# Cosine-weighted linear attention followed by a multiplicative FFN on one core: hand-written instruction order, 1 KB load runs and casting weight loads in place of a scheduled program

## Chip, cores, metric

The kernel runs on one core of one Trainium2 chip. The metric is the device time of one execution in microseconds (us); a run of the kernel before is given as the median of three executions. The page of the profile shows one profiled execution, whose times count from its first instruction.

## What is computed

q, k and v have 8 batches, 8 heads, 576 rows of 64. phi(x) is max(x,0) times a cosine weight, and the same times a sine weight, side by side (128 features); the weights depend on the row.

```python
kv  = einsum('bhsf,bhsd->bhfd', phi(k), v);  z = sum(phi(k), axis=2)
x   = (phi(q) @ kv) / (phi(q) @ z + 1e-6)          # -> 4608 tokens x 512
out = ((x @ w1) * (x @ w2)) @ w3 @ w_out           # 512 -> 1024 -> 1024 -> 512, fp32
```

## The kernel before

Matmuls run in bf16. First the weights are prepared: w1, w2, w_out and w3 are loaded in fp32 by SP's queue (L82 to L96) into the pool `wstage`, cast to bf16 by DVE and ACT, w3 is transposed by PE block by block (L101), and w34b = w3 @ w_out is multiplied out (L106) and evicted by ACT (L108). Then the pool `wstage` is closed, and the pools of the attention (`ld`, `phi` and so on) are opened in its place.

`attention(b)` works in five chunks of rows (128, 128, 128, 128, 64). Per chunk, q is loaded by SP's queue (L131) and k and v by POOL's (L132, L133), in runs of 256 bytes (one row of one head). DVE makes the cosine halves (L137, L141), ACT the sine halves (L139, L143), and v is cast into `va` beside a column of ones (L145, L146). PE transposes the eight heads of phi(q) (L151), and DVE copies them to `qpT` (L152). Then PE sums kv over the chunks (L160), ACT and DVE evict it, and per chunk PE multiplies phi(q) by it (L173), DVE divides (L176 to L183), PE transposes the result (L188), and it is copied into `xT4`, all tokens' transposed x (L190).

`ffn(t)` takes 512 tokens: for each of eight column blocks four matmuls with w1 (L199), four with w2 (L202), an ACT copy of the first (L205) and a DVE product (L206); then four output blocks of eight matmuls each (L210), an ACT copy (L213) and a store from ACT's queue. The tiles `ffnps` have two buffers, which the two groups of a block take in turn:

```python
ps_ffn = ctx.enter_context(tc.tile_pool(name="ps_ffn", bufs=2, space=bass.MemoryType.PSUM))
...
            aT = ps_ffn.tile([P, 512], FP32, name="ffnps")
            bT = ps_ffn.tile([P, 512], FP32, name="ffnps")
```

The program is attention(0), ffn(0), attention(1), ffn(1), ..., attention(7), ffn(7), ffn(8), but the order on each engine is set by the scheduler of the language, which may draw instructions forward; engines then run their queues in order.

Of the kernel before, what the change touches and what calls it, by code (L numbers as in the profile page):

```python
# [42 lines left out]
def kernel(  # L43
# [34 lines left out]
    w34b = wpool.tile([P, 8, DM], BF16, name="w34b")

    with tc.tile_pool(name="wstage", bufs=1) as wst:  # L80
        wf1 = wst.tile([P, 4, DFF], FP32, name="wf1")
        nc.sync.dma_start(out=wf1[:], in_=moe_w1.rearrange("(c p) j -> p c j", p=P))  # L82
        nc.vector.tensor_copy(out=w1b[:, 0:2, :], in_=wf1[:, 0:2, :])
        nc.scalar.copy(out=w1b[:, 2:4, :], in_=wf1[:, 2:4, :])
        wf2 = wst.tile([P, 4, DFF], FP32, name="wf2")
        nc.sync.dma_start(out=wf2[:], in_=moe_w2.rearrange("(c p) j -> p c j", p=P))
        nc.vector.tensor_copy(out=w2b[:, 0:2, :], in_=wf2[:, 0:2, :])
        nc.scalar.copy(out=w2b[:, 2:4, :], in_=wf2[:, 2:4, :])
        wouts = wst.tile([P, 8, DM], FP32, name="wouts")
        nc.sync.dma_start(out=wouts[:], in_=moe_w_out.rearrange("(c p) m -> p c m", p=P))  # L90
        woutb = wst.tile([P, 8, DM], BF16, name="woutb")
        nc.any.tensor_copy(out=woutb[:], in_=wouts[:])
        w3T = wst.tile([P, 8, DFF], BF16, name="w3T")
        for jc in range(8):
            w3f = wst.tile([P, DFF], FP32, name="w3f", bufs=2)
            nc.sync.dma_start(out=w3f[:], in_=moe_w3[ts(jc, P), :])  # L96
            w3c = wst.tile([P, DFF], BF16, name="w3c", bufs=2)
            nc.any.tensor_copy(out=w3c[:], in_=w3f[:])  # L98
            pstage = ps_qt.tile([P, 8, 128], BF16, name="pst")
            for lc in range(8):  # L100
                nc.tensor.transpose(pstage[:, lc, :], w3c[:, ts(lc, 128)], identb[:])  # L101
            nc.any.tensor_copy(out=w3T[:, :, ts(jc, 128)], in_=pstage[:])
        for jp in range(8):
            ps34 = ps_ffn.tile([P, 512], FP32, name="ffnps")
            for lc in range(8):
                nc.tensor.matmul(ps34[:, :], lhsT=w3T[:, lc, ts(jp, 128)],  # L106
                                 rhs=woutb[:, lc, :], start=(lc == 0), stop=(lc == 7))
            nc.scalar.copy(out=w34b[:, jp, :], in_=ps34[:, :])  # L108

    xtpool = ctx.enter_context(tc.tile_pool(name="xt", bufs=1))  # L110
    xT4 = xtpool.tile([P, 4, T], BF16, name="xT4")

    ld = ctx.enter_context(tc.tile_pool(name="ld", bufs=3))
    phi = ctx.enter_context(tc.tile_pool(name="phi", bufs=6))
    qtp = ctx.enter_context(tc.tile_pool(name="qtp", bufs=2))
    xb = ctx.enter_context(tc.tile_pool(name="xb", bufs=8))
    sm = ctx.enter_context(tc.tile_pool(name="sm", bufs=4))
    ffnsb = ctx.enter_context(tc.tile_pool(name="ffn", bufs=2))

    def attention(b):  # L120
# [134 lines left out]
```

## Time and profile before

| | us |
|---|---|
| runs (three) | 365.64, 366.74, 370.58; median 366.74 |
| span of the profiled execution | 364.5 |
| PE busy | 295.6 (81%) |
| DVE, ACT, POOL busy | 171.1, 169.8, 72.6 |

No separate time is given for the profiled execution; its span is 2.2 us below the median of the runs. [...] An interval of a few microseconds may show more than one engine busy with the same work, since matmuls are pipelined.

### The profile page before, as it was taken

What the parts mean: (1) busy time and instruction counts of PE and PEld (TensorE: products, weight loads), DVE (VectorE), ACT (ScalarE), POOL (GpSimd) and SP (SyncE); (2) the same over time, 40 slices, a digit from 0 to 9 for tenths busy, and PEclk for the clock granted to TensorE, in tenths of its full rate; (3) what the DMA queues carried; (4) which work ended last, traced back from release to release, by engine and by line L of the source; (5) the groups of instructions that cost most, each with busy time, mean ns of one, the idle gap of its engine ahead of it and who ended that gap; (6) DMA issues with size and microseconds to landing.
All of it is one profiled execution on the core that took longest, in us unless ns stands there. A gap on an engine that the chain in (4) does not pass through costs nothing.

```text
span 364.5 us, 5583 instructions
## 1 busy us (share of the span) xinstructions
PE 295.6 (81%) x2085; PEld 157.5 (43%) x2112; DVE 171.1 (47%) x476; ACT 169.8 (47%) x276; POOL 72.6 (20%) x107
## 2 busy tenths in 40 slices
PE   0059722572999779999999999999899999899996
PEld 0034322462345544474455446446445544544442
DVE  2322043765530867269429617826742732742230
ACT  2376342545533756368339437736542332332322
POOL 0000161433310735216206402801000000000000
PEclk9999955555899859999999999999999999899999
DMA  8975099999923699537934933882102002001103
GB/s 300 397 270 185 22 227 197 201 219 170 177 61 115 151 218 167 150 112 186 178 116 124 227 99 103 187 175 101 32 0 97 22 0 108 9 0 48 69 0 115
DMA packets 51851, 48.60 MB, mean 133 GB/s; under 512 B 39536, under 2 KB 39536, under 8 KB 51824
## 3 DMA queue, kind: packets, MB, share of 16 engines
q1 hardware_dynamic: 40752, 19.93, 24.3%
q0 software_dynamic: 5888, 18.88, 23.3%
q10 hardware_dynamic: 5184, 9.44, 6.9%
q8 instruction: 16, 0.26, 0.4%
q14 instruction: 11, 0.09, 0.1%
HBM read 38.80 MB, written 9.44 MB: 132 GB/s over the span
## 4 chain that ended last, share of the span: by engine, by line
PE 62%; DMA 22%; DVE 6%; ACT 4%; SPq 2%; issue 2%; ACTq 0%; DVEq 0%; POOL 0%; POOLq 0%
PE ffnps L202 17%; PE ffnps L210 16%; PE ffnps L199 16%; DMA qs<-in_q_dram 12%; DMA w3f<-in_moe_w_dram 6%; PE kvA L160 3%; PE xst L188 2%; PE pst L151 2%; PE kvB L160 2%; SPq L96 2%; PE ffnps L106 2%; DVE qpT L152 1%; DMA ks<-in_k_dram 1%; ACT qp L143 1%; DMA vs<-in_v_dram 1%
## 5 line engine op out<-in xcount | busy, mean ns | idle before, releaser
L199 PE MATMUL ffnps<-xT,w1b 128*128 128x512 bf16 x275 | 76.1, 387 | 6.3 <-ACT asb L205 1.8
L206 DVE TENSOR_TENSOR abT<-asb,ffnps 128x512 bf16<-128x512 bf16 x72 | 49.3, 685 | 65.9 <-PE ffnps L202 60.2
L202 PE MATMUL ffnps<-xT,w2b 128*128 128x512 bf16 x280 | 76.9, 384 | 0.4 <-DVE abT L206 0.2
L205 ACT CAST asb<-ffnps 128x512 bf16<-128x512 f32 x72 | 42.1, 584 | 60.6 <-PE ffnps L199 59.0
L210 PE MATMUL ffnps<-w34b,abT 128*128 128x512 bf16 x284 | 63.4, 379 | 0.3
L132 POOL DMA_DIRECT2D ks<-in_k_dram x40 | 35.3, 884 | 84.3 <-ACT w34b L108 42.5
L151 PE MATMUL pst<-identb,qp 128*128 128x128 bf16 (+1 forms) x320 | 29.9, 237 | 19.0 <-DVE qpT L152 9.6
L213 ACT COPY osb<-ffnps 128x512 f32<-128x512 f32 x36 | 21.1, 587 | 51.3 <-PE ffnps L210 45.5
L210 PEld LDWEIGHTS <-abT 128*128 128x128 bf16 x288 | 28.2, 98 | 34.0
L202 PEld LDWEIGHTS <-w2b 128*128 128x128 bf16 x288 | 26.8, 98 | 35.6 <-issue 12.9
L199 PEld LDWEIGHTS <-w1b 128*128 128x128 bf16 x288 | 27.4, 99 | 33.7 <-issue 6.0
L143 ACT ACTIVATE qp<-qs,sinv 128x512 bf16<-128x512 f32 (+1 forms) x40 | 28.9, 721 | 24.4 <-DMA qs<-in_q_dram 20.8
L133 POOL DMA_DIRECT2D vs<-in_v_dram x40 | 34.9, 874 | 21.2 <-ACT va L145 10.3
L152 DVE COPY qpT<-pst 128x1024 bf16<-128x1024 bf16 (+1 forms) x40 | 25.1, 627 | 17.7 <-PE pst L151 17.5
L151 PEld LDWEIGHTS <-qp 128*128 128x128 bf16 (+1 forms) x320 | 22.6, 108 | 24.8 <-issue 10.3
L139 ACT ACTIVATE kp<-ks,sinv 128x512 bf16<-128x512 f32 (+1 forms) x40 | 28.3, 718 | 3.7 <-DMA ks<-in_k_dram 2.7
L188 PE MATMUL xst<-identb,xblk 128*128 128x128 bf16 (+1 forms) x160 | 22.7, 230 | 8.0 <-DVE xblk L180 7.7
L141 DVE TENSOR_SCALAR qp<-qs,cosv 128x512 bf16<-128x512 f32 (+1 forms) x40 | 19.9, 500 | 16.0 <-DMA qs<-in_q_dram 15.8
L160 PEld LDWEIGHTS <-kp 128*128 128x128 bf16 (+1 forms) x320 | 20.4, 102 | 15.4 <-issue 7.5
L137 DVE TENSOR_SCALAR kp<-ks,cosv 128x512 bf16<-128x512 f32 (+1 forms) x40 | 20.8, 519 | 11.5 <-PE kvB L160 8.5
L101 PE MATMUL pst<-identb,w3c 128*128 128x128 bf16 x64 | 5.7, 242 | 23.4 <-DVE w3c L98 21.9
L190 ACT COPY xT<-xst 128x512 bf16<-128x512 bf16 (+1 forms) x26 | 13.8, 532 | 17.9 <-PE xst L188 17.9
(49 smaller groups left out, 243.2 us busy)
## 6 DMA issues: line engine op xcount, KB each, us to landing
out_dram<-osb ACTq DMA_DIRECT2D x36, 256.0 KB, 2.0
qs<-in_q_dram SPq DMA_DIRECT2D x32, 256.0 KB, 5.7
ks<-in_k_dram POOLq DMA_DIRECT2D x32, 256.0 KB, 5.9
vs<-in_v_dram POOLq DMA_DIRECT2D x32, 256.0 KB, 6.5
wf<-in_moe_w_dram SPq DMA_DIRECT2D x2, 2048.0 KB, 9.8
w3f<-in_moe_w_dram SPq DMA_DIRECT2D x8, 512.0 KB, 4.1
wouts<-in_moe_w_out_dram SPq DMA_DIRECT2D x1, 2048.0 KB, 17.0
qs<-in_q_dram SPq DMA_DIRECT2D x8, 128.0 KB, 7.0
```

The costliest lines, as they stand in the source:

```text
L132: nc.gpsimd.dma_start(out=ks[:Rc], in_=k[b, :, s0:s0 + Rc, :].rearrange("h s d -> s h d"))
L133: nc.gpsimd.dma_start(out=vs[:Rc], in_=v[b, :, s0:s0 + Rc, :].rearrange("h s d -> s h d"))
L143: nc.scalar.activation(out=qp[:Rc, :, D:F], in_=qs[:Rc], func=ACTF.Relu, scale=sinv[:Rc, c:c + 1], bias=0.0)
L151: nc.tensor.transpose(pst[:, h, 0:Rc], qp[:Rc, h, :], identb[:Rc, :Rc])
L152: nc.vector.tensor_copy(out=qpT[:, :, s0:s0 + Rc], in_=pst[:, :, 0:Rc])
L160: nc.tensor.matmul(slot, lhsT=kps[c][:Rc, h, :], rhs=vas[c][:Rc, h, :], start=first, stop=last)
L188: nc.tensor.transpose(xst[:, kc, 0:Rc], xblk[:Rc, 2 * kc:2 * kc + 2, :], identb[:Rc, :Rc])
L199: nc.tensor.matmul(aT[:, :], lhsT=w1b[:, kc, ts(jc, 128)], rhs=xT4[:, kc, cols], start=(kc == 0), stop=(kc == 3))
L202: nc.tensor.matmul(bT[:, :], lhsT=w2b[:, kc, ts(jc, 128)], rhs=xT4[:, kc, cols], start=(kc == 0), stop=(kc == 3))
L205: nc.scalar.copy(out=asb[:], in_=aT[:, :])
L206: nc.vector.tensor_mul(out=abT[:, jc, :], in0=asb[:], in1=bT[:, :])
L210: nc.tensor.matmul(ops[:, :], lhsT=abT[:, jc, ts(ms, 128)], rhs=w34b[:, jc, :], start=(jc == 0), stop=(jc == 7))
```

## The change

The order of every engine's instructions is now as the code is written (`tc.manual_schedule()`), and the code is written so that pieces of attention(t+1) stand between the 24 groups of four matmuls of ffn(t). A batch has 25 pieces: five `prep` (no PE work), five kv chunks, five transposes of phi(q), five `num`, five `x_tr`. In tile 0 they begin with the ninth group. attention(0) stands alone ahead of ffn(0). The first 512 rows of a batch are dealt to chunks as rows 4p+j, so that a load run is 1 KB; k, v and q are loaded per batch by SP's queue, one batch ahead; stores leave SP's queue too. The weights come by POOL's queue and are cast by the transfer; w3 @ w_out is made in two halves with `prep(0)` between. `ffnps` has four buffers; the attention's PSUM tile `pnum` has one. v is cast by POOL. The load pool no longer lies where the weights are staged.

```diff
-    ps_ffn = ctx.enter_context(tc.tile_pool(name="ps_ffn", bufs=2, space=bass.MemoryType.PSUM))
+    ld = ctx.enter_context(tc.tile_pool(name="ld", bufs=2))
...
+    ps_ffn = ctx.enter_context(tc.tile_pool(name="ps_ffn", bufs=4, space=bass.MemoryType.PSUM))
+    ps_att = ctx.enter_context(tc.tile_pool(name="ps_att", bufs=1, space=bass.MemoryType.PSUM))
+    ps_tr = ctx.enter_context(tc.tile_pool(name="ps_tr", bufs=2, space=bass.MemoryType.PSUM))
+    ctx.enter_context(tc.manual_schedule())
...
+    for i in range(4):
+        nc.gpsimd.dma_start(out=w3b[:, 0:4, ts(i, 256)], in_=w3v[:, 0:4, ts(i, 256)])
+        nc.gpsimd.dma_start(out=woutb[:, ts(i, 2), :], in_=wov[:, ts(i, 2), :])
...
+    for i in range(2):
+        nc.gpsimd.dma_start(out=w3b[:, 4:8, ts(i, 512)], in_=w3v[:, 4:8, ts(i, 512)])
+    cosv, sinv = _trig_tables(nc, const)
...
+    def load(b):
+        for name, src in (("k", k), ("v", v), ("q", q)):
+            t = ld.tile([P, H, 4, D], FP32, name=name + "s")
+            nc.sync.dma_start(out=t[:], in_=src[b, :, 0:512, :].rearrange("h (p j) d -> p h j d", j=4))
+            t4 = ld.tile([64, H, D], FP32, name=name + "s4")
+            nc.sync.dma_start(out=t4[:], in_=src[b, :, 512:S, :].rearrange("h p d -> p h d"))
...
+    load(0)
+    for i in range(4):
+        nc.gpsimd.dma_start(out=w1b[:, :, cs], in_=w1v[:, :, cs])
+        nc.gpsimd.dma_start(out=w2b[:, :, cs], in_=w2v[:, :, cs])
+    load(1)
...
+    def w34_half(half):
+        for lc in range(8):
+            for jp in range(4):
+                nc.tensor.transpose(pst[:, jp, :], w3b[:, 4 * half + jp, ts(lc, 128)], identb[:])
+            if lc % 2:
+                nc.scalar.copy(out=w3T[:], in_=pst[:, 0:4, :])
+            else:
+                nc.vector.tensor_copy(out=w3T[:], in_=pst[:, 0:4, :])
+            if prev is not None:
+                mms(*prev)
...
+        nc.gpsimd.tensor_copy(out=va[:R, c, :, 0:D], in_=vs)
...
+    def attention_units(b):
+        order = [0, 1, 2, 3, 4] if b % 2 == 0 else [4, 0, 1, 2, 3]
+        u = [(lambda c=c: kv_chunk(b, c)) for c in range(NCH)]
+        u.insert(2, lambda: q_tr(b, order[0]))
+        u.insert(5, lambda: q_tr(b, order[1]))
+        for i in range(NCH + 1):
+            if i < NCH:
+                u.append(lambda c=order[i]: num(b, c))
+            if i + 2 < NCH:
+                u.append(lambda c=order[i + 2]: q_tr(b, c))
+            if i >= 1:
+                u.append(lambda c=order[i - 1]: x_tr(b, c))
...
+    w34_half(0)
+    for c in range(NCH):
+        prep(0, c)
+    w34_half(1)
...
+    for u in attention_units(0):
+        u()
+    for t in range(NT):
+            if b + 1 < B:
+                load(b + 1)
+            first = 8 if t == 0 else 0
+            pr = [(lambda c=c: prep(b, c)) for c in range(NCH)]
+            at = attention_units(b)
+            todo = pr[0:2] + [f for p in zip(pr[2:], at[0:3]) for f in p] + at[3:]
+            per = len(todo) / (n - first)
```

`num` is the product with kv and the division (now three DVE instructions of 128x8, 128x8 and 128x512), `x_tr` the transposes of its result with an ACT copy. A matmul or an eviction of the FFN has the same form as before.

Three places show how the instructions moved. At the start of POOL's queue (w3b, woutb, w1b, w2b are the bf16 weights, s_i the row numbers for the weights of phi) there stood before, from the identity matrix on:

```order
L21 IOTA s_i 128x5
masks.py:197 MEMSET identb 128x128
masks.py:199 AFFINE_SELECT identb<-identb 128x128
L132 DMA ks<-in_k_dram 128x8x64
L133 DMA vs<-in_v_dram 128x8x64
```

and now, behind seven weight transfers and the identity matrix:

```order
L95 DMA woutb<-in_moe_w_out_dram 128x2x512
L99 DMA w3b<-in_moe_w_dram 128x4x512 x2
L26 IOTA s_i 128x4
L27 IOTA s_i 128x1
L106 MEMSET va_137 128x40
L106 MEMSET va_139 128x40
L123 DMA w1b<-in_moe_w_dram 128x4x256
L124 DMA w2b<-in_moe_w_dram 128x4x256
```

The row numbers are now made behind ten transfers, and k and v have left this queue. On DVE, at the end of the tables of cosines and sines, there stood before

```order
L38 TENSOR_TENSOR sinv<-sinv,th 128x5
L87 CAST w2b<-wf_120 128x2048
L98 CAST w3c<-w3f 128x1024 x3
L102 COPY w3T<-pst 128x8x128
L98 CAST w3c<-w3f 128x1024 x4
L146 MEMSET va 128x8
L141 TENSOR_SCALAR qp<-qs,cosv 128x8x64
```

and now

```order
L44 TENSOR_TENSOR sinv<-sinv,th 128x5
L145 COPY w3T<-pst 128x512 x4
L155 CAST w34b<-ffnps 128x512 x2
L175 TENSOR_SCALAR kp<-ks,cosv 128x8x64
L179 TENSOR_SCALAR qp<-qs,cosv 128x8x64
```

The casts of weights are gone, and the first copy of transposed w3 stands behind the tables. On ACT, between two tiles of the FFN (asb and osb are the FFN's evictions, kp and qp the sine halves of phi), there stood before

```order
L163 CAST kvs<-kvA 128x260
L143 ACTIVATE qp<-qs,sinv 128x8x64 x2
L139 ACTIVATE kp<-ks,sinv 128x8x64
L190 COPY xT_325<-xst 128x4x128
L145 CAST va<-vs 128x8x64 x3
L190 COPY xT_325<-xst 128x4x128
L139 ACTIVATE kp<-ks,sinv 128x8x64 x2
L205 CAST asb<-ffnps 128x512
```

and now, within a tile,

```order
L281 CAST asb<-ffnps 128x512
L177 ACTIVATE kp<-ks,sinv 128x8x64
L181 ACTIVATE qp<-qs,sinv 128x8x64
L281 CAST asb<-ffnps 128x512
L177 ACTIVATE kp<-ks_595,sinv 64x8x64
L181 ACTIVATE qp<-qs_603,sinv 64x8x64
L281 CAST asb<-ffnps 128x512 x2
L201 CAST kvs<-pnum 128x260
L281 CAST asb<-ffnps 128x512 x2
```

An eviction of the FFN now stands behind two or four activations of the next batch, and the casts of v are gone.

## Rows read from the trace of the kernel before

**Rows 1.** The page's 40 slices: PE's busy tenths; GB/s moved.

```profile
PE   0059722572999779999999999999899999899996
...
GB/s 300 397 270 185 22 227 197 201 219 170 177 61 115 151 218 167 150 112 186 178 116 124 227 99 103 187 175 101 32 0 97 22 0 108 9 0 48 69 0 115
```

**Rows 2.** Windows: us, busy (count) of PE, PEld, DVE, ACT, POOL; clock; DMA; GB/s.

```profile
20.00:43.40 23.40, 19.77 (x126) 10.60 (x128) 5.55 (x8) 14.31 (x17) 0.00 (x0) 1.00 0.44 146
43.40:92.00 48.60, 19.84 (x190) 15.82 (x191) 25.49 (x76) 21.71 (x34) 20.13 (x23) 0.53 1.13 198
92.00:361.00 269.00, 255.96 (x1769) 131.06 (x1793) 134.69 (x366) 127.02 (x223) 51.68 (x77) 0.97 0.43 104
188.30:198.00 9.70, 8.88 (x122) 6.35 (x121) 8.49 (x29) 8.38 (x15) 3.93 (x9) 1.00 0.43 125
```

**Rows 3.** Timeline of POOL at its first load: start, us, what, [idle <-releaser].

```profile
43.96 1.02 POOL L132 DMA_DIRECT2D ks<-in_k_dram  x1 [42.49 <-ACT w34b L108]
```

**Rows 4.** DMA queues, first 0 to 43.4 us, then 43.4 to 92 us.

```profile
q1 hardware_dynamic: 3248, 10.49, 66.5%
...
q1 hardware_dynamic: 17320, 4.36, 60.6%
q0 software_dynamic: 1616, 5.21, 52.0%
```

**Rows 5.** Timeline of PE within ffn(0).

```profile
97.24 1.03 PE L199 MATMUL ffnps<-xT,w1b 128*128 128x512 bf16 x4
98.25 1.02 PE L202 MATMUL ffnps<-xT,w2b 128*128 128x512 bf16 x4
99.11 1.03 PE L199 MATMUL ffnps<-xT,w1b 128*128 128x512 bf16 x4
```

**Rows 6.** Chain that ended last, output matmuls of one tile.

```profile
273.13 6.91 PE ffnps L210 x32
```

**Rows 7.** Groups by form: names, count | busy, mean ns | idle before, releasers.

```profile
L206 DVE TENSOR_TENSOR abT<-asb,ffnps 128x512 bf16<-128x512 bf16 x72 | 49.3, 685 | 65.9 <-PE ffnps L202 60.2 <-PE ffnps L199 3.6 <-ACT asb L205 1.1
L205 ACT CAST asb<-ffnps 128x512 bf16<-128x512 f32 x72 | 42.1, 584 | 60.6 <-PE ffnps L199 59.0 <-DVE den L178 0.8 <-PE ffnps L202 0.5
L132 POOL DMA_DIRECT2D ks<-in_k_dram x40 | 35.3, 884 | 84.3 <-ACT w34b L108 42.5 <-ACT kp L139 14.6 <-ACT asb L205 6.7
...
L139 ACT ACTIVATE kp<-ks,sinv 128x512 bf16<-128x512 f32 x32 | 22.5, 717 | 3.2 <-DMA ks<-in_k_dram 2.2 <-PE kvB L160 1.0
L152 DVE COPY qpT<-pst 128x1024 bf16<-128x1024 bf16 x32 | 21.7, 679 | 10.9 <-PE pst L151 10.8
...
L180 DVE TENSOR_TENSOR xblk<-numA,den 128x256 bf16<-128x256 f32 x32 | 13.4, 418 | 0.3
...
L178 DVE RECIPROCAL den<-den 128x8 f32<-128x8 f32 x32 | 6.2, 195 | 0.3
...
L32 DVE TENSOR_SCALAR cosv<-cosv 128x5 f32<-128x5 f32 x5 | 0.9, 170 | 0.0
...
masks.py:199 POOL TENSOR_SCALAR_AFFINE_SELECT identb<-identb 128x128 bf16<-128x128 bf16 x1 | 0.3, 295 | 0.1
...
masks.py:197 POOL MEMSET identb<- 128x128 bf16 x1 | 0.2, 200 | 0.0
```

**Rows 8.** Timeline of PE: one chunk's transposes, half of one chunk's products.

```profile
118.07 0.62 PE L151 MATMUL pst<-identb,qp 128*128 128x128 bf16 x8
...
118.52 0.29 PE L173 MATMUL numA<-kvs,qpT 128*128 128x65 bf16 x4
```

**Rows 9.** DVE's cosine half of q: durations, min, median, max.

```profile
L141 DVE TENSOR_SCALAR qp<-qs,cosv x40: 426/478/896, 46.8 to 265.1; 128x512 bf16<-128x512 f32 x32, 64x512 bf16<-64x512 f32 x8
```

**Rows 10.** Timeline of PE: eight transposes of w3, early and later.

```profile
20.86 1.03 PE L101 MATMUL pst<-identb,w3c 128*128 128x128 bf16 x8 [20.86 <-DVE w3c L98]
...
26.31 0.61 PE L101 MATMUL pst<-identb,w3c 128*128 128x128 bf16 x8
```

More of the change, by code (lines that the diff above doesn't have):

```diff
@@ L78 @@
[L78 to L108, printed above, removed]
@@ new lines, with x_tr @@
+    xT = {}
+    def x_tr(b, c):
+        R = ROWS[c]
+        xblk = att[b]["x"].pop(c)
+        xf = xblk[:R].rearrange("p g h d -> p (g h d)")
+        if b % 2 == 0:
+            slot = S * b + 128 * c
+        else:
+            slot = S * b + (0 if c == 4 else 64 + 128 * c)
+        t, o = divmod(slot, 512)
+        if t not in xT:
+            xT[t] = xtp.tile([P, 4, 512], BF16, name="xT")
+        pst = ps_tr.tile([P, 8, 128], BF16, name="pst")
+        for kc in range(4):
+            nc.tensor.transpose(pst[:, kc, 0:R], xf[:, ts(kc, 128)], identb[:R, :R])
+        nc.scalar.copy(out=xT[t][:, :, ds(o, R)], in_=pst[:, 0:4, 0:R])
@@ L195, in ffn, with out_rows, ffn_groups @@
+    def out_rows(g):
+        pair, r = divmod(g, 9)
+        b0 = 2 * pair
+        if r == 4:
+            return [(64 * i, 64, out[ds((b0 + i) * S + 512, 64), :]) for i in range(2)]
+        b, j = (b0, r) if r < 4 else (b0 + 1, r - 5)
+        return [(0, 128, out[ds(b * S, 512), :].rearrange("(p j) m -> p j m", j=4)[:, j, :])]
+    def ffn_groups(t):
+        x = xT[t]
+        abT = fsb.tile([P, 8, 512], BF16, name="abT", bufs=2)
         for jc in range(8):
             aT = ps_ffn.tile([P, 512], FP32, name="ffnps")
+            for kc in range(4):
+                nc.tensor.matmul(aT[:, :], lhsT=w1b[:, kc, ts(jc, 128)], rhs=x[:, kc, :],
+                                 start=(kc == 0), stop=(kc == 3))
+            asb = fsb.tile([P, 512], BF16, name="asb")
+            nc.scalar.copy(out=asb[:], in_=aT[:, :])
+            yield
@@ L197, in ffn @@
             bT = ps_ffn.tile([P, 512], FP32, name="ffnps")
             for kc in range(4):
[L199 removed]
+                nc.tensor.matmul(bT[:, :], lhsT=w2b[:, kc, ts(jc, 128)], rhs=x[:, kc, :],
                                  start=(kc == 0), stop=(kc == 3))
[L201 to L203 removed]
@@ L204, in ffn @@
-            asb = ffnsb.tile([P, 512], BF16, name="asb")
-            nc.scalar.copy(out=asb[:], in_=aT[:, :])
             nc.vector.tensor_mul(out=abT[:, jc, :], in0=asb[:], in1=bT[:, :])
+            yield
         for ms in range(4):
```

269 lines of the change are left out of this document (149 added, 120 removed).

## Prediction

> **What bounds the kernel now.** I read the page's slices first, then busy time by stage, then the timeline where a stage begins and the DMA queues of each stage, and last the groups by form, for prices. In the slices (9.1 us each) the reader sees PE idle in the first two, half busy up to the tenth, and at nine tenths or more in most of the rest [rows 1]. By stage [rows 2]: from 20.0 to 43.4 us the weights are prepared, PE busy 19.8 of 23.4 us. From 43.4 to 92.0 us, where ffn(0) begins, PE is busy 19.8 of 48.6 us at a granted clock of 0.53, nearly always the lower of its levels, while the DMA engines' share is 1.13 (packets overlap, so every engine has work all the time): this stage waits for transfers. From 92.0 to 361.0 us PE is busy 256.0 of 269.0 us at 0.97: PE bounds it. So what can be had lies mostly in the first 92 us; behind them only 13 us are idle.
>
> The second stage starts late because POOL's first load of k waits 42.5 us for the last eviction of w34b [rows 3]: the load tiles lie where the weights were staged. It is slow because of its runs of 256 bytes. While active, SP's queue moved 4.36 MB in 60.6% of 48.6 us, 148 GB/s, and POOL's 5.21 MB in 52.0%, 206 GB/s; the weights before moved 10.49 MB in 66.5% of 43.4 us, 363 GB/s [rows 4].
>
> In the last stage a pair of groups of ffn(0) starts at 97.24 us and the next at 99.11, 1.87 us for eight matmuls [rows 5], where 32 output matmuls take 6.91 us, 0.216 each [rows 6], or 1.73 for eight. The other 0.14 us is the w2 group's wait for a free `ffnps` buffer: with two buffers it needs the product of the pair before, which takes DVE 0.685 us and follows PE [rows 7].
>
> **The change, part by part.** I build the time anew: the start of ffn(0), then PE's work, then the tail.
>
> *Transfers ahead of ffn(0).* Both batches that SP issues at once and POOL's weights share the engines. Ahead of the last piece of w3 stand 4.2 MB of w3, 2.1 MB of w_out and 7.1 MB of q, k, v. A packet of q (252 bytes on average) took 0.606*48.6*16/17320 = 27.2 ns of one engine, one of the weights (3230 bytes) 0.665*43.4*16/3248 = 142 ns [rows 4]. On the line between them 1 KB takes 57 ns (287 GB/s over 16 engines) and 2 KB 97 ns (339 GB/s). So 8.4 MB in 1 KB runs take 29 us, 4.2 MB in 2 KB runs 12, 0.8 MB of 64-row chunks in 256 B runs 5, and the start about 2 (300 against 397 GB/s in the first two slices [rows 1]): w3 is complete at 49 us. That a cast in the transfer costs nothing is not shown by any row. Its ends are 363 and 206 GB/s for POOL's 6.3 MB, the two rates nearest to it; I take the line, since the runs are like those of no row.
>
> *Work under them.* POOL issues ten transfers at 0.88 us [rows 7] ahead of the row numbers, so DVE's tables (27 instructions of 0.17 us or a little over) end at about 15 us, and the first half of w34 starts there, not with its data. ACT's ten activations of `prep(0)`, 7.2 us at 0.717 [rows 7], stand between the halves. Both lie beside the transfers. Behind the last piece of w3 come four rounds of the second half, each of four transposes and four long matmuls: 1.2 us at full clock, nearly twice that at half (eight transposes took 1.03 us early and 0.61 later [rows 10]). At 1.7 us that is 7 us, to 56.
>
> *attention(0)* stands alone. Seven pieces of eight matmuls at 0.6 us [rows 8] and the eviction of kv make 5 us. Then `pnum` has one buffer, so the next `num` waits for the division of the one before: 0.6 us of PE, then add and reciprocal (0.2 each) and a product of 512 elements, for which I take 0.7 (0.418 for 256, nearly all by the element [rows 7]), with handovers 2.0 us. Five of them make 10. ffn(0) starts at 71 us instead of 92. Bounds: were transfers free, DVE's tables, 16 rounds at 1.2, `prep` and attention(0) would still need 15+19+7+15 = 56; with casts at 206 GB/s w3 is complete at 2+25+31 = 58 us, and ffn(0) starts at 80. What was hidden for nothing before, the casts of weights on ACT and DVE, goes, and is worth nothing by itself.
>
> *PE's work from there.* The FFN is 9 tiles of 24 groups at 4*0.216 = 0.864 us, 186.6 us; four buffers remove the 0.14 us per pair, 72 times, 10 us. A batch of attention has 60 transposes at 0.62/8 and 80 products at 0.29/4 us [rows 8], 10.4 us. From below: the last stage has 1769 matmuls [rows 2], 905 of them not of the FFN's 864, of 140 per batch 6.5 batches; 256.0 - 9*(8*1.87+6.91) = 59 us, 9.1 each. I take 9.6, and seven batches are 67 us. For waits at the seams, of which before had 13 us, I take 6.
>
> *The tail* behind PE's last matmul, from 361.0 us to the span's end at 364.5, stays: 3.5 us.
>
> Sum: 71 + 186.6 + 67 + 6 + 3.5 = 334 us of span, against 364.5. The span lies 2.2 us below the median of the runs, so 336 us against 366.74.
>
> *What must stay hidden.* At the head of a tile ACT gets ten activations (7.2 us) and four evictions (2.3 us) in seven groups and their pieces, about 7.2 us of PE: it falls 2.3 us behind. Four buffers let PE run three groups ahead, 2.6 us, so the cover is thin but holds. POOL's cast of v is in no row. Between a memset of 128 elements at 0.20 us (more elements can't take less) and a select of 128 elements at 0.295 [rows 7], 512 elements take 0.2 to 1.2 us; I take 0.8. Five of them end before the chunks' products are due, some 2 us apart. Loads of a batch are issued a tile (30 us) ahead and need 13 us.
>
> **The rivals.** *A: the cast makes the transfer slow.* For it: no row shows one, and q, k, v now take bandwidth from the weights. Against it: POOL's queue held 206 GB/s beside SP's. At half of that, 103, w3 is complete at 2+25+61 = 88, ffn(0) starts at 110, and waits 9 us more for the last chunk of w1 and w2 (4.2 MB, 41 us, to 129): 336+39+9 = 384, slower. It loses against before once w3 lands later than 49+31 = 80 us, which is a cast stream under 119 GB/s; at 206 it gives 345.
>
> *B: queues in order make PE wait in the mixed tiles.* For it: the thin cover on ACT, one `pnum` buffer, DVE's product of the FFN behind `prep`. DVE's cosine halves took 0.43 to 0.90 us [rows 9], so something can nearly double them. Against it: by the prices of rows 7 and 9, ACT has twelve evictions, ten activations and six copies of about 0.5, some 17 us, and DVE eight products, ten halves, five copies and five divisions, some 20, of 30 us per tile. At 2 us more per tile the time is 350, at 5 us 371; from 3.3 us per tile on no gain beyond 2% is left. [...]
>
> *C: the front part stays at half clock.* [...] The trace doesn't bear it out for this mix: in 188.3 to 198.0 us, 122 matmuls, 8.88 us of PE in all and so nearly all of them small, ran at 1.00 [rows 2]. But the stage at 0.53 was one with PE half idle, and w34 with attention(0) is that too. Four rounds at 2.2 and attention(0)'s PE part doubled add 9 us: 345.
>
> **How the numbers follow.** The forecast has 0.64; its own range, 322 to 350, takes ffn(0)'s start from 61 to 80 us, with 9.1 to 10.4 us per batch. A has 0.12 (a third of it the slower end), B 0.16, C 0.08. The time is the forecast's, 336 us. For 8 in 10 the range reaches to B's middle and A's milder end, 318 to 358. About 2% (359.4 us) is what a measurement can tell from no change. Faster: 0.63 of the forecast, 0.06 of A, 0.09 of B, all of C: 0.86. Within 2%: 0.08, from B and A. Slower: 0.06, from A's end and B's.
>
> **What would show it.** Right: SP's first loads at the start and not at 43 us; the last transfer of w3 landing near 49 us; PE's first FFN matmul at 65 to 77; pairs of groups without pieces 1.73 us apart in the last two tiles; 30 to 31 us from tile to tile in between at clock 1.00. Wrong: PE waiting for POOL's transfers beyond 60 us (A), for ACT's asb or POOL's va in every mixed tile (B), clock 0.5 up to ffn(0) with the transfers done (C). A start of ffn(0) at 71 with a time over 350 would mean that the steady tiles are mispriced, not the front.

## The result, and the profile after

The changed kernel takes 308.24 us (median of four runs, 308.13 to 308.85) against 366.50 of the kernel before on the same chip: 0.839 of its time, 95% interval 0.834 to 0.843. The forecast of faster was right, the 336 us were 28 too many, and the time lies below the range of 318 to 358. One of the four runs of the first woven front (the last experiment), its profiled one, lay 1.6% above the fastest and is left out of its median, and no start of ffn(0) is read from it.

By stage (columns as in [rows 2]; the stage up to 55.2 us answers to the first 92 us of [rows 2], the rest to its long third row; a clock of 1.00 is full speed by the profile):

```profile
0.00:55.20 55.20, 29.90 (x266) 17.44 (x268) 22.73 (x69) 16.83 (x28) 20.39 (x38) 0.93 1.18 234
58.00:88.00 30.00, 25.88 (x199) 13.89 (x201) 16.94 (x33) 12.57 (x23) 3.42 (x5) 0.88 0.35 93
...
118.00:148.00 30.00, 27.95 (x241) 15.22 (x244) 18.80 (x42) 16.20 (x29) 2.84 (x5) 1.00 0.63 161
148.00:178.00 30.00, 29.74 (x248) 16.13 (x252) 18.40 (x41) 18.10 (x33) 2.84 (x5) 1.00 0.63 166
```

ffn(0) begins at 55.25 us (timeline of PE) instead of 92.0. Up to there the clock is 0.93 in the mean, not 0.53 as in the second stage before (0.50 in each of its windows from 50 us on). Then PE is busy nearly all the time: a window in which an even batch is worked in (148 to 178) has 0.26 us idle, one with an odd batch (118 to 148) 2.05. The start of the program, in PE's timeline:

```profile
17.02 1.89 PE L133 MATMUL ffnps<-woutb,w3T 128*128 128x512 bf16 x4 [7.82 <-DVE w3T L145]
...
25.31 1.93 PE L133 MATMUL ffnps<-woutb,w3T 128*128 128x512 bf16 x8
28.41 0.62 PE L140 MATMUL pst<-identb,w3b 128*128 128x128 bf16 x8 [1.18 <-DMA w3b<-in_moe_w_dram]
32.39 1.89 PE L133 MATMUL ffnps<-woutb,w3T 128*128 128x512 bf16 x4 [3.35 <-DVE w3T L145]
...
38.05 0.39 PE L140 MATMUL pst<-identb,w3b 128*128 128x128 bf16 x4
...
41.53 1.93 PE L133 MATMUL ffnps<-woutb,w3T 128*128 128x512 bf16 x8
43.30 0.68 PE L196 MATMUL pnum<-va,kp 128*128 128x65 bf16 x16
...
55.25 0.61 PE L278 MATMUL ffnps<-xT,w1b 128*128 128x512 bf16 x1
```

The reader sees four stages: the first half of w34 (17.0 to 27.2), a gap in which DVE and ACT make the features of batch 0, the second half (32.4 to 43.5) and attention(0) (to 55.2). When their data came is seen in the DMA queues from 2 to 33 us, and in the issues of SP and POOL (for an issuing queue, the second column is how long the issue took):

```profile
q0 software_dynamic: 4420, 3.23, 66.3%
q1 hardware_dynamic: 5396, 4.25, 52.5%
```

```profile
17.53 6.87 SPq L116 DMA_DIRECT2D ks<-in_k_dram  x1
...
25.25 8.65 SPq L116 DMA_DIRECT2D vs<-in_v_dram  x1
...
32.87 0.74 POOL L124 DMA_DIRECT2D w2b<-in_moe_w_dram  x1 [3.46 <-DMA w3b<-in_moe_w_dram]
```

q0 are POOL's casting transfers: their bytes are counted as written (bf16), so 3.23 MB were 6.46 MB read (in the whole span q0 has 5.24 MB for the weights, which came as 10.49 MB before [rows 4]). q1 is SP's. Two of SP's issues took 7 to 9 us each while transfers were under way, so that until 33 us only 4.25 MB of q, k, v were moved, and the last issue in POOL's row that waits for w3 is released at 32.87 us. The second half did not wait for that last piece: PE waited until 32.39 us for DVE, whose order puts the features of batch 0 (27.8 to 31.9) ahead of the first copy of transposed w3, and the rounds that use the last piece began only at 38.05.

### The profile page after: what moved, and what is told of

The parts are those of the page before. It is cut to its first block, busy times and chain, and to the rows that moved or that the text cites. A ratio compares the mean times of both kernels' runs of the same rounds, so it can differ in the third digit from the quotient of the medians.

```text
span 306.4 us, 5315 instructions
## 1 busy us (share of the span) xinstructions
PE 265.0 (86%) x2074; PEld 141.8 (46%) x2112; DVE 160.2 (52%) x358; ACT 141.5 (46%) x249; POOL 38.0 (12%) x68
## 3 DMA queue, kind: packets, MB, share of 16 engines
q0 software_dynamic: 8480, 5.24, 11.5%
## 4 chain that ended last, share of the span: by engine, by line
PE 77%; ACT 9%; DVE 6%; issue 4%; DMA 3%; POOL 0%; ACTq 0%; POOLq 0%
PE ffnps L292 20%; PE ffnps L278 18%; PE ffnps L285 17%; PE ffnps L133 6%; PE pst L210 6%; ACT qp L181 4%; PE pnum L218 4%; PE pnum L196 3%; ACT kp L177 3%; DMA woutb<-in_moe_w_out_dram 3%; PE pst L244 2%; ACT asb L281 2%; DVE xblk L225 1%; PE pst L140 1%; DVE kp L175 1%
## 5 line engine op out<-in xcount | busy, mean ns | idle before, releaser
L292 PE MATMUL ffnps<-w34b,abT 128*128 128x512 bf16 x275 | 69.7, 379 | 0.7
L178 POOL CAST va<-vs 128x512 bf16<-128x512 f32 (+1 forms) x40 | 23.3, 626 | 164.1 <-DMA vs<-in_v_dram 138.4
L245 ACT COPY xT<-pst 128x512 bf16<-128x512 bf16 (+1 forms) x40 | 21.7, 544 | 30.4 <-PE pst L244 30.4
L292 PEld LDWEIGHTS <-abT 128*128 128x128 bf16 x288 | 25.0, 98 | 21.3
L210 PE MATMUL pst<-identb,qp 128*128 128x128 bf16 (+1 forms) x320 | 23.4, 217 | 8.8 <-ACT qp L181 8.8
L133 PE MATMUL ffnps<-woutb,w3T 128*128 128x512 bf16 x62 | 19.8, 451 | 11.2 <-DVE w3T L145 11.2
L225 DVE TENSOR_TENSOR xblk<-pnum,den 128x512 bf16<-128x512 f32 (+1 forms) x40 | 27.6, 689 | 1.4
L210 PEld LDWEIGHTS <-qp 128*128 128x128 bf16 (+1 forms) x320 | 18.8, 99 | 16.6 <-ACT qp L181 10.8
L218 PEld LDWEIGHTS <-qpT 128*128 128x128 bf16 (+1 forms) x320 | 14.4, 100 | 15.5 <-DVE xblk L225 6.5
L222 DVE TENSOR_SCALAR den<-pnum 128x8 f32<-128x8 f32 (+1 forms) x40 | 6.5, 163 | 28.1 <-PE pnum L218 28.1
L218 PE MATMUL pnum<-kvs,qpT 128*128 128x65 bf16 (+1 forms) x320 | 17.0, 194 | 4.0 <-DVE xblk L225 2.9
L196 PEld LDWEIGHTS <-kp 128*128 128x128 bf16 (+1 forms) x320 | 15.1, 99 | 10.5 <-issue 4.1
## 6 DMA issues: line engine op xcount, KB each, us to landing
vs<-in_v_dram SPq DMA_DIRECT2D x8, 1024.0 KB, 11.5
qs<-in_q_dram SPq DMA_DIRECT2D x8, 1024.0 KB, 10.7
vs<-in_v_dram SPq DMA_DIRECT2D x8, 128.0 KB, 11.5
```

Source lines behind the costliest of these rows:

```text
L133: nc.tensor.matmul(acc[jp][:, :], lhsT=w3T[:, ts(jp, 128)], rhs=woutb[:, lc, :], start=(lc == 0), stop=(lc == 7))
L210: nc.tensor.transpose(pst[:, h, 0:R], qp[:R, c, h, :], identb[:R, :R])
L218: nc.tensor.matmul(nt[:R, h // 4, ds((h % 4) * 65, 65)], lhsT=qpT[:, h, ds(128 * c, R)], rhs=kvs[:, h, :], start=True, stop=True)
L225: nc.vector.tensor_tensor(out=xblk[:R], in0=n4[:, :, :, 0:D], in1=den[:R].unsqueeze(3).to_broadcast([R, 2, 4, D]), op=ALU.mult)
L292: nc.tensor.matmul(ops[:, :], lhsT=abT[:, jc, ts(ms, 128)], rhs=w34b[:, jc, :], start=(jc == 0), stop=(jc == 7))
```

## The experiments

All runs with a time stand beside the kernel before; the changed kernel's ratio to it is 0.839. Differences in us are of medians. ffn(0)'s start and the distance of tiles are read from PE's timeline (first matmul with w1 of a tile).

### Odd batches in the order of their rows

An odd batch takes its chunks in the order 4, 0, 1, 2, 3, but its features and kv chunks stand in the order 0 to 4: the last feature is the first that is transposed.

```diff
-            pr = [(lambda c=c: prep(b, c)) for c in range(NCH)]
+            pr = [(lambda c=c: prep(b, c)) for c in ([0, 1, 2, 3, 4] if b % 2 == 0 else [4, 0, 1, 2, 3])]
...
-        u = [(lambda c=c: kv_chunk(b, c)) for c in range(NCH)]
+        u = [(lambda c=c: kv_chunk(b, c)) for c in order]
```

> In batches 1, 3, 5, 7 the first piece that transposes phi(q) is of chunk 4, whose activations ACT does last; the trace of the changed kernel has PE waiting 8.8 us in all there, four times. Here the odd batches prepare and sum chunk 4 first. Theory (these waits are real and nothing stands behind them): 308.2 - 8.8 = about 299.5 us, and the four waits gone. Rival (ACT is simply late at the head of a tile, and PE then waits at the next piece instead): 306 to 308 us.

296.71 us, ratio 0.808 [0.803, 0.813]: 11.5 us less than the changed kernel, more than the waits. Why it is more is seen in the changed kernel's PE timeline and windows behind the first of these waits:

```profile
72.39 0.60 PE L210 MATMUL pst<-identb,qp 64*128 64x64 bf16 x8 [3.80 <-ACT qp L181]
72.92 1.89 PE L285 MATMUL ffnps<-xT,w2b 128*128 128x512 bf16 x4
74.61 0.65 PE L196 MATMUL pnum<-va,kp 128*128 128x65 bf16 x8
...
77.21 1.04 PE L210 MATMUL pst<-identb,qp 128*128 128x128 bf16 x8
```

```profile
68.00:72.40 4.40, 0.60 (x4) 0.11 (x3) 2.90 (x7) 4.33 (x8) 0.00 (x0) 0.94 0.00 0
72.40:76.00 3.60, 3.60 (x23) 1.86 (x24) 1.11 (x2) 0.00 (x0) 0.00 (x0) 0.50 0.02 5
```

After the 3.8 us of idleness four long matmuls take 1.7 us from start to next instead of 0.86: the granted clock is 0.50 in the window's row, and the same work takes some 2 us more up to 77.21. In this run the same window is at 1.00. Tile 0 got 5.7 us shorter (36.64 to 30.95), each of the three later tiles with an odd batch 1.6 (28.94 to 27.30), where the wait was 1.7 and the clock did not fall (1.00 from 126 to 130 us, around the first of them). Another 0.5 us lies ahead of ffn(0).

### Two buffers for the FFN's sums

`ps_ffn` has two buffers again, and for that two of the four sums of w34 lie in the two halves of a `pnum` tile.

```diff
-    ps_ffn = ctx.enter_context(tc.tile_pool(name="ps_ffn", bufs=4, space=bass.MemoryType.PSUM))
+    ps_ffn = ctx.enter_context(tc.tile_pool(name="ps_ffn", bufs=2, space=bass.MemoryType.PSUM))
...
-        acc = [ps_ffn.tile([P, 512], FP32, name="ffnps") for _ in range(4)]
+        two = ps_att.tile([P, 2, 512], FP32, name="pnum")
+        acc = [ps_ffn.tile([P, 512], FP32, name="ffnps") for _ in range(2)] + [two[:, 0, :], two[:, 1, :]]
```

> ffnps has two buffers instead of four (half of the sums for w34 lie in the attention's PSUM tile for that). Theory (the four buffers save what the prediction priced, 0.14 us per pair of groups): 72 pairs, +10 us, 318 us, a little less where a piece covers the wait. Rival (the buffers are also the cover for ACT, which falls behind by 2.3 us and more at the head of a tile): +10 and 3 to 5 us in each of seven tiles, 340 to 355 us. Other rival (pieces between the groups hide the wait everywhere but in the last two tiles): 311 us.

315.81 us, ratio 0.861 [0.854, 0.868]: 7.6 us more than the changed kernel. A pair of groups without pieces, here (tile 7) and in the changed kernel (tile 8):

```profile
271.26 1.03 PE L279 MATMUL ffnps<-xT,w1b 128*128 128x512 bf16 x4
272.27 1.02 PE L286 MATMUL ffnps<-xT,w2b 128*128 128x512 bf16 x4
273.13 1.03 PE L279 MATMUL ffnps<-xT,w1b 128*128 128x512 bf16 x4
```

```profile
285.02 1.03 PE L278 MATMUL ffnps<-xT,w1b 128*128 128x512 bf16 x4
285.88 1.03 PE L285 MATMUL ffnps<-xT,w2b 128*128 128x512 bf16 x4
286.74 1.03 PE L278 MATMUL ffnps<-xT,w1b 128*128 128x512 bf16 x3
```

1.87 us with two buffers, 1.72 with four: the forecast's 0.14 per pair, seen alone. That is 1.0 us in each of the last two tiles. In tiles with a batch it is 0.9 us (even) and 0.3 (odd, where PE waits for ACT anyhow), and tile 0 is 0.6 shorter, so over the program the two buffers cost 5.0 us and not 10. The other 2.0 us lie ahead of ffn(0), where the sums of w34 now share `pnum`: that is a price of the edit's second part and not of the FFN's buffers. The bigger loss, ACT falling behind in each tile, didn't come: PE waited 5.0 us in all for `asb`.

### Attention behind the FFN, not between

No piece is placed between the groups; the loop that the kernel has behind them then places all 25 at the tile's end.

> attention(t+1) stands behind ffn(t) on every engine, not between its groups; nothing else is changed. Theory (the pieces' answers from DVE and ACT are hidden by FFN groups): a batch alone takes 12.4 us as attention(0) does, and 2 to 3 us more for the first chunks of prep, against 8.6 us per tile between groups: +6 to 7 us in each of seven tiles, 350 to 357 us. Rival (placement matters little, the kernel before had only 13 us of idle PE with most of its attention apart from the FFN): at most +13, 321 us.

```diff
-                want = min(len(todo), int(round((g + 1 - first) * per)))
+                want = 0
```

398.36 us, ratio 1.086 [1.078, 1.093]: slower than before, and 90 us slower than the changed kernel, twice what the waits alone let expect. One batch alone, and the ffn behind it:

```profile
122.10:138.50 16.40, 11.40 (x140) 9.10 (x142) 8.62 (x21) 8.51 (x15) 2.10 (x4) 0.62 0.82 215
138.50:141.70 3.20, 3.20 (x8) 1.22 (x8) 0.00 (x0) 0.67 (x2) 0.74 (x2) 0.50 0.42 98
```

From its first matmul a batch takes 16.4 us alone, PE idle 5 of them, at a clock of 0.62, and the FFN's first eight matmuls still run at 0.50. Between FFN groups the same pieces ran at 1.00 (the changed kernel's windows from 118 to 178 us). So laying the pieces between the groups saves their waits and here also kept the clock; how much of the 90 us either makes was not measured apart. Whether the low clock of the batch alone comes from its idle time or from its small matmuls, this run doesn't show.

### Runs of 256 bytes again

Chunks of 128 consecutive rows, in four transfers per load.

```diff
-            nc.sync.dma_start(out=t[:], in_=src[b, :, 0:512, :].rearrange("h (p j) d -> p h j d", j=4))
+            for j in range(4):
+                nc.sync.dma_start(out=t[:, :, j, :], in_=src[b, :, ts(j, 128), :].rearrange("h p d -> p h d"))
...
```

The row numbers of the tables and the rows of the stores follow.

> Chunks are again blocks of 128 rows, so q, k, v are loaded in runs of 256 bytes, by four transfers where there was one. Theory (steady tiles hide 3.5 MB at 148 GB/s, 24 of 30 us; in the front the 4.2 MB that stand beside w3 take 28 instead of 16 us): w3 is complete 8 to 12 us later, and the time is 313 to 320 us. Rival (the front is bound by the engines' order, which has slack against the transfers): under 311 us. Rival on the other side (loads don't keep up with the tiles): over 330 us.

325.59 us, ratio 0.887 [0.881, 0.892]: 17.4 us more, all of it ahead of ffn(0) (72.98 instead of 55.25 us), and none in the tiles, whose distances stay within 0.02 us (27.37, 28.95), but for tile 0, which is 0.24 shorter. DMA queues from 2 to 51 us, and the longest waits of PE and, up to 73 us, of DVE:

```profile
q0 software_dynamic: 8480, 5.24, 72.1%
q1 hardware_dynamic: 16612, 4.18, 56.1%
```

```profile
PE ffnps L134 <- DVE w3T L146: 31.0, 2, 23.0
...
DVE qp L180 <- DMA qs<-in_q_dram: 17.8, 4, 16.3
```

All 5.24 MB of the weights were through by then, but SP had moved only 4.18 MB in 49 us, batch 0's 3.5 and little more. It is now not w3 that is late, as the theory had it, but q: DVE waits 16.3 us for it in one piece, its features of batch 0 stand ahead of the copies of transposed w3 in half 1, and PE waits 23.0 us behind them.

### Tables first; batch 1's loads later; batch 1's loads at once

Three runs on the transfers. In the first the tables are made ahead of the weights' issues:

```diff
     identb = const.tile([P, P], BF16, name="identb")
+    cosv, sinv = _trig_tables(nc, const)
     for i in range(4):
...
-    cosv, sinv = _trig_tables(nc, const)
```

> The cosine and sine tables are made ahead of the weight transfers in POOL's and VectorE's order; nothing else moves. In the changed kernel VectorE makes the tables from 11.5 to 16.6 us, behind POOL's ten transfer issues, and TensorE waits 7.8 us for the first evicted w3 tile. Order theory: this wait is what holds half 0 back, so half 0 starts near 11 us instead of 17, ffn(0) at 49 instead of 55.3, and the kernel takes about 302 us. Rival, transfers: half 0 ends with the last w_out piece (landed at 25.25, its matmuls at 25.31), half 1 with the last w3 piece (32.8); these do not move, so ffn(0) stays within 1 us of 55.3 and the time at 307 to 308 us. The POOL issues come some 1 to 2 us later than now, so the transfers may even land later: up to 310.

308.76 us, ratio 0.839 [0.832, 0.845]: nothing. The wait only changes its name. PE's waits up to 60 us, here and in the changed kernel:

```profile
PE pst L140 <- DMA w3b<-in_moe_w_dram: 13.9, 5, 9.5
PE ffnps L133 <- DVE w3T L145: 3.7, 1, 3.7
```

```profile
PE ffnps L133 <- DVE w3T L145: 11.2, 2, 7.8
PE pst L140 <- DMA w3b<-in_moe_w_dram: 9.3, 2, 8.2
```

Half 0 starts earlier, waits for its weights piece by piece, and ends no earlier: its evictions on DVE begin at 28.29 us, in the changed kernel at 26.63.

In the second, batch 1's loads are issued only behind half 0, held there by a write of one element into each tile on DVE:

```diff
-    load(1)
...
     w34_half(0)
+    load(1, held=True)
```

> Batch 1's q/k/v loads are issued behind half 0 of w3@w_out instead of at the start, held there by a write of one element into each tile on VectorE. Theory of the forecast (the front is set by the bytes of both batches' loads ahead of w3): half of these bytes leaves the stretch before 33 us; the window from 2 to 33 us moved 4.25 MB of q/k/v of which about 0.7 MB belonged to batch 1, so at the stretch's 340 GB/s w3 and w_out come some 2 to 4 us earlier by the bytes counted here, and 12 us earlier if the whole of batch 1 stood ahead as the forecast had it: 296 to 306 us. Rival: the front is set by the casting transfers of POOL alone, or by the order on VectorE; then less than 2 us is gained (306 to 310), and attention(1) still starts on time, since its first prep comes at about 75 us.

309.99 us, ratio 0.843 [0.835, 0.851]: no gain, though the transfers did come earlier: POOL's row that waits for w3 is released at 30.98 us instead of 32.87, as the counted bytes let expect. There was little to gain, since in the changed kernel half 1 waits for DVE and not for the last piece of w3 (above), as the rival of VectorE's order had it. And DVE got slower. POOL got free earlier, and its five casts of v fell into DVE's features:

```profile
31.04 0.47 DVE L174 TENSOR_SCALAR kp<-ks,cosv 128x512 bf16<-128x512 f32 x1
31.43 3.50 DVE L178 TENSOR_SCALAR qp<-qs,cosv 128x512 bf16<-128x512 f32 x1
```

```profile
31.81 2.84 POOL L177 CAST va<-vs 128x512 bf16<-128x512 f32 x5
```

An instruction of 0.47 us stood for 3.50, to the end of the casts, and half 1 started 3.7 us later (36.11). In the changed kernel the casts ran from 33.6 us, behind DVE's last feature.

In the third, ScalarE's queue issues batch 1's loads at the start, so that they don't stand behind SP's:

```diff
-    load(1)
+    load(1, nc.scalar)
```

> The changed kernel with batch 1's q/k/v loads issued by ScalarE's queue at the start, so that they no longer stand behind batch 0's in SP's issue order: all 7.1 MB of both batches run beside w3, as the forecast had it. In the changed kernel 4.25 MB of q/k/v and 6.46 MB of weights (read as fp32) went in 31 us, 345 GB/s, and the last piece of w3 landed at 32.9 us. Theory of the bytes: 2.8 MB more ahead of w3 cost 2.8/0.345 = 8 us: w3 complete at 41, ffn(0) at 63 instead of 55.3, the kernel 316 us. Rival, each queue has a share of its own: POOL's queue keeps its rate and w3 moves by less than 2 us, 307 to 310 us; or a third queue takes a third of the engines, POOL's stream falls from 208 to 140 GB/s or less, w3 is complete near 48, and the kernel takes 323 us or more.

315.68 us, ratio 0.854 [0.848, 0.861], ffn(0) at 63.99 us, and w3 is complete at 42.10: the theory of the bytes, to about a microsecond. DMA queues from 2 to 41 us (q10 is ScalarE's), POOL's row that waits for w3, and what held half 0 (an issue of ScalarE's queue, and two waits of PE):

```profile
q0 software_dynamic: 4373, 3.21, 52.2%
q1 hardware_dynamic: 4688, 3.52, 36.4%
q10 hardware_dynamic: 4699, 3.54, 28.1%
```

```profile
42.10 0.74 POOL L125 DMA_DIRECT2D w2b<-in_moe_w_dram  x1 [2.55 <-DMA w3b<-in_moe_w_dram]
...
16.90 7.17 ACTq L117 DMA_DIRECT2D qs<-in_q_dram  x1
20.59 1.89 PE L134 MATMUL ffnps<-woutb,w3T 128*128 128x512 bf16 x4 [8.11 <-DVE w3T L146]
26.03 1.89 PE L134 MATMUL ffnps<-woutb,w3T 128*128 128x512 bf16 x4 [3.12 <-ACT w3T L144]
```

With the cast bytes as read, 2*3.21 + 3.52 + 3.54 = 13.5 MB in 39 us are 346 GB/s; in the changed kernel 6.46 + 4.25 = 10.7 MB in 31 us, 345. By the bytes as written the two would be 263 and 241. So in these runs the queues share one rate, a cast takes its part by the bytes read, and the order of the issues decides whose bytes come first. That the kernel's time agrees as well is in part luck: the last piece of w3 was not awaited here either (its first use is at 46.40 us). Half 0 was late: it began 3.6 us later, as DVE's tables ended at 20.2 us instead of 16.6, and then waited 3.1 us for a copy on ScalarE, which stood behind its own issues of the loads until 24.09. That second price comes from the queue chosen and not from the bytes.

### The pieces twice

Each transposing matmul of q and x and each product of the numerator is issued twice.

```diff
-            nc.tensor.transpose(pst[:, h, 0:R], qp[:R, c, h, :], identb[:R, :R])
+            for _ in range(2):
+                nc.tensor.transpose(pst[:, h, 0:R], qp[:R, c, h, :], identb[:R, :R])
...
```

> Each transposing matmul of q and x and each product of the numerator is issued twice into the same place, so the output is unchanged; per batch that adds 60 transposes and 40 products on TensorE. By the pitch in the changed kernel's mixed tiles (55 ns per transpose, 33 ns per product) a batch gains 60 x 0.055 + 40 x 0.033 = 4.6 us, seven mixed tiles 32 us, attention(0) another 3 to 5: about 343 us. By the price of the forecast (0.62 us per 8 transposes, 0.29 per 4 products, that is 0.0775 and 0.0725 each) a batch gains 7.5 us and the kernel 53 + 7: about 368 us.

336.80 us, ratio 0.915 [0.909, 0.922]: 28.6 us more, near the 35 of the pitch and far from the 60 of the forecast's price. Starts of tiles 3 and 4, here and in the changed kernel:

```profile
160.28 1.03 PE L281 MATMUL ffnps<-xT,w1b 128*128 128x512 bf16 x4
...
191.81 1.04 PE L281 MATMUL ffnps<-xT,w1b 128*128 128x512 bf16 x4
```

```profile
148.21 1.03 PE L278 MATMUL ffnps<-xT,w1b 128*128 128x512 bf16 x4
...
175.58 1.04 PE L278 MATMUL ffnps<-xT,w1b 128*128 128x512 bf16 x3
```

31.53 against 27.37 us: 100 matmuls more cost 4.16 us, 42 ns each in the mean. Odd batches gain 4.2 us too; tile 0, where PE waits most, gains only 1.7, which is why the sum stays below 35.

### The casts of v on ScalarE

```diff
-        nc.gpsimd.tensor_copy(out=va[:R, c, :, 0:D], in_=vs)
+        nc.scalar.copy(out=va[:R, c, :, 0:D], in_=vs)
```

> The changed kernel with one part undone: the 45 casts of v go on ScalarE (a row of ScalarE's features of the same size takes 0.71 us) instead of POOL (0.61 to 0.81 us). Theory that POOL hides them for nothing but ScalarE could not: ScalarE gets 0.71 x 5 = 3.6 us more in each batch, and in the four odd batches, where TensorE already waits 3.8 to 8.8 us in all for ScalarE's last feature, the wait grows by up to 3.6 us each: 314 to 323 us. Rival: ScalarE (142 of 306 us busy) has room, and VectorE's features no longer stand beside POOL's casts (0.83 us there instead of 0.48): 303 to 308 us.

329.51 us, ratio 0.900 [0.894, 0.906]: 21.3 us more, beyond the theory's end. PE's waits of the whole span:

```profile
PE pst L210 <- ACT qp L181: 18.4, 4, 5.5
```

It was 8.8 us in the changed kernel. The later tiles with an odd batch became 33.1 us long (28.94), together 12.5 us more, and again more than the wait: their windows have the clock at 0.94. Another 3.8 us lie ahead of ffn(0), which the theory did not count, 1.6 in tile 0, and 0.85 in each even tile.

### The kernel before with its load tiles apart

One edit in the kernel before: the pool of q, k and v is opened ahead of the weights' staging, so the loads needn't wait for its memory [rows 3].

```diff
+    ld = ctx.enter_context(tc.tile_pool(name="ld", bufs=3))
+
...
-    ld = ctx.enter_context(tc.tile_pool(name="ld", bufs=3))
```

> The kernel before, with one edit: the pool of the q/k/v tiles is opened ahead of the staging pool of the weights, so that its tiles do not lie in memory that the w3 staging must give back. In the kernel before, the first q/k/v transfer was issued only behind the front (TensorE's chain went from the front to the loads, and ffn(0) began at 92.0 us). Theory that the front's loss was the loads waiting for the staging's memory: ffn(0) starts 20 to 28 us earlier and the kernel takes 338 to 347 us. Rival: the fp32 staging and VectorE's casts set the front, and the loads were hidden: 362 to 367 us.

358.90 us, ratio 0.975 [0.966, 0.983]: 7.3 us, between the two theories. ffn(0) starts at 86.39 us, 5.6 earlier, the stage ahead of it still runs at the lower clock, and POOL's wait did not go (a window's row, and POOL's timeline):

```profile
60.00:80.00 20.00, 11.09 (x112) 9.08 (x112) 9.60 (x29) 9.59 (x16) 6.53 (x8) 0.50 1.12 200
...
51.97 0.13 POOL L147 MEMSET va<- 128x8 bf16 x1 [44.86 <-PE ffnps L108]
```

Six of POOL's loads now go out at the start, but the tiles of the features (`kp`, `qp`, `va`) still lie where the weights were staged, and behind those six POOL waits 44.86 us again. The run thus prices only the loads' part of that wait; what the features' part cost is not shown. The weights were done later too, at 51.9 us instead of 43.3.

### A front woven together

Two versions on top of the odd batches' order: the tables first, k's features between the rounds of half 0, the casts of v ahead of most of w1 and w2, and attention(0) between the rounds of half 1; in the second also batch 1's loads behind half 0.

```diff
-    w34_half(0)
-    for c in range(NCH):
-        prep(0, c)
-    w34_half(1)
+    w34_half(0, [[part(c, "k")] if c < NCH else [] for c in range(8)])
...
+    w34_half(1, [[part(2, "q"), at[0]], [part(3, "q"), at[1], at[2]], [part(4, "q"), at[3]], [at[4], at[5]],
+                 [at[6]], [at[7], at[8]], at[9:11], at[11:13]])
```

> Odd batches in the order of their rows (as in the run with that edit alone, 296.7 us), and a front in another order: the tables first, k's features between the rounds of half 0, the casts of v ahead of most of the w1 and w2 transfers, and q's features and attention(0) between the rounds of half 1 instead of behind it. Theory: in the changed kernel the front from 25 us on is a chain of stages that leave each other's engines idle (features 27.8 to 31.9, half 1 to 43.2, attention(0) to 55.2); laid beside each other they are bound by VectorE's work, some 12 us, behind the last piece of w3 at 28 to 33 us, so ffn(0) starts at 43 to 47 us instead of 54.8 and the kernel takes 285 to 289 us. Rival: w1 and w2, issued later, land last (their transfers are now behind the casts of v), and ffn(0) waits for them: 292 to 300 us.

> The woven front, and batch 1's q/k/v loads held until half 0 is done, so that w3, w1 and w2 have the transfers' rate to themselves and batch 0. The run with this edit alone brought the last w3 piece from 32.9 to 31.0 us, but there VectorE stood 3.5 us in one instruction beside POOL's casts of v. Theory: without that collision the 2 us count, 1 to 3 us below the woven front alone (283 to 288 us); if the w1 and w2 transfers bound the woven front, 3 to 6 below it. Rival: attention(1) gets its inputs too late (its first features are due in ffn(0)'s ninth group, some 15 us behind ffn(0)'s start): 2 to 6 us above it.

289.44 us, ratio 0.791 [0.784, 0.797], and 289.82, ratio 0.792 [0.788, 0.797]: both beat the changed kernel by 18 to 19 us and the order of odd batches alone by 7, and they can't be told apart. In the second, ffn(0) starts at 46.87 us; the theory of the first had 43 to 47. The times lie above what was expected, by up to 4 us in the first and 2 to 7 in the second. The chain of the second version at the end of the front:

```profile
41.59 0.69 DVE xblk L233
42.28 1.20 DVE w34b L160 x2
```

The work of attention(0) that was left behind half 1 stands on DVE, and DVE's evictions of w34b, 1.2 us, stand in the middle of it.

## Why the prediction was wrong

The parts of its sum are those that the time is made of, but three terms had the wrong size, and the last piece of w3 no longer set the front as it had in the forecast. By its steps, in us of span (334 forecast, 306.4 measured):

**Transfers ahead of ffn(0): "w3 is complete at 49 us". It was complete at 33, and this is the first step that failed.** It failed twice. The forecast put all 7.1 MB of both batches ahead of the last piece of w3; SP's issues were held up, so only 4.25 MB went ahead. And the rate was 345 GB/s, not the 291 (13.4 MB in 46 us) of the line between two kinds of packet. The run with batch 1's loads on a second queue shows both: with all the bytes beside w3 it was complete at 42, so the order of issues was worth some 9 us and the rate the other 7. That a cast in the transfer needs no price of its own was right (345 and 346 GB/s with the cast bytes as read). With w3 complete at 33, half 1 waited for DVE instead (its rounds with the last piece began at 38.05), whose features of batch 0 the forecast had put beside the transfers.

**Work under the transfers, and attention(0).** "Four rounds behind the last piece of w3, 7 us" were eight, from 32.4 to 43.5, since the features of batch 0 (27.8 to 31.9 on DVE) stood ahead of half 1 and not beside the transfers: 4 us more. attention(0) took 12 us and not 15, since a step of the numerator took 1.65 and not 2.0. These two nearly cancel; ffn(0) started at 55.25 instead of 71, 15.75 us too early for the forecast.

**PE's work.** The FFN is right: the last two tiles take 20.72 and 20.9 us, nine of them 186.6, and the four buffers are worth the 0.14 us per pair where no piece stands between (5.0 us in all, not 10, by the run with two). The batch is the second step that failed: "I take 9.6". An even tile takes 27.37 us, so a batch adds 6.6, and seven 46.5 instead of 67, 20.5 less. The price came from rows like "0.62 us per eight transposes" [rows 8], and such a row runs from the first matmul's start to the last one's end. What counts is the distance to the next instruction. The two rows of [rows 8] have it: the second begins 0.45 us behind the first. So it is in the changed kernel's timeline:

```profile
132.00 0.61 PE L210 MATMUL pst<-identb,qp 128*128 128x128 bf16 x8
132.45 0.81 PE L285 MATMUL ffnps<-xT,w2b 128*128 128x512 bf16 x3
```

The run with the pieces twice weighs them in the time: 42 ns per matmul, where the forecast had 75. The forecast's bound from below, 9.1, was shared out from the third stage's busy time, which takes such rows at their whole length wherever PE idles behind them and has a clock of 0.97; how much either adds was not measured.

**Seams: 6 us. The third step that failed, the other way.** PE lost about 14: 10.6 in the odd batches (by the run that mends their order) and some 3.5 more in tile 0. In that run 2.4 of these lie at ffn(0)'s start, whose first two pairs take 5.9 us instead of 3.5 at a granted clock of 0.58; the rest stays open. The forecast looked for waits at ACT's evictions at the head of a tile, where the cover of four buffers held, and not at the order of features against that of transposes, which the code shows.

By luck this hides a part of the two other misses. Together: 334 - 15.75 - 20.5 + 8 + 0.5 (the tail was 4.0) = 306.3.

**The rivals.** A fell: POOL's cast stream kept 6.46 MB in 31 us, 208 GB/s, beside SP's. B came true in a small way: PE waited 1.7 us in odd tiles (3.8 in the first), for one operand in the wrong order and not for a queue's thin cover. C fell for the front as a whole (0.93), yet the lower clock came back: behind the 3.35 us of idle PE ahead of half 1 it was 0.50 from 32.39 to 36.80, and the first eight long matmuls of half 0, from 17.02 us, came at half their later pace (1.7 and 1.6 us per four, later 0.86), though the record has 1.00 there. POOL's casts held up DVE's features, for which the forecast's sum has no term: beside casts DVE's 0.48 us became 0.83 in tile 0, and 3.50 when batch 1's loads were held. No wait of PE in the changed kernel's tiles goes back to it (8.8 us of waits there are for ScalarE's feature), while on ScalarE the casts cost 21 us.

## What to carry to other kernels

- Price small matmuls by the distance from one instruction's start to the next one's, never by a row's length (here 42 ns, where the forecast had 75), and long idle stretches of PE (here 3.4 and 3.8 us, not 1.7) by their length plus the slower matmuls behind them.
- In a front that waits for transfers, count the bytes that are issued ahead of the one awaited, as the queues will really issue them (here 4.25 of 7.1 MB of q, k, v), and expect a wait that is taken from another engine to reappear as a wait for data (with the tables first, PE's waits for DVE's copies of transposed w3 fell from 11.2 to 3.7 us and those for w3 rose from 9.3 to 13.9).
- Where an order is written out by hand, lay the order in which operands are made beside the order in which they are used: here that was worth 11 us.

## What the runs showed of the hardware

- Behind 3.80 us of idle PE the granted clock was 0.50 from 72.40 to 76.00 us, PE busy all the time; behind 1.69 us, in the later tiles with an odd batch, it stayed 1.00.
- One DVE instruction stood 3.50 us beside five POOL casts in a row (2.84 us), until the last had ended; in tile 0 of the changed kernel three of DVE's instructions took 0.83 us apiece (0.48 alone) and POOL's casts up to 0.81 (0.61). In the first the DVE instruction began ahead of the casts (31.43 against 31.81 us) and still waited for all five. In the second DVE's instructions came every 0.75 us, where one of DVE's and one of POOL's in turn (0.39 and 0.56 from start to start when alone) would take 0.95, so there the two ran in part at the same time.
- A casting transfer took its part of the rate by the bytes it reads: 345 and 346 GB/s in two runs with different shares of cast and plain bytes, where the bytes as written would make 241 and 263.
- Transposes of 128 x 128 and products of 65 columns came every 42 ns in the mean at full clock (100 more in 4.16 us, at a granted clock of 1.00), while their rows say 0.2 us each (217 and 194 ns in the mean on the changed kernel's page).
